# A retention layer and a squared-relu network in one kernel: the list scheduler that orders all instructions is given VectorE's rate beside GpSimd and new lags, and one constant is made elsewhere

## The chip, the cores and the metric

The kernel runs on one core of one Trainium2 chip. The metric is the device time of one execution in microseconds (us). A core has five engines with a queue of instructions each: PE (TensorE, matrix products), DVE (VectorE), ACT (ScalarE), POOL (GpSimd) and SP (SyncE, which here only issues DMA transfers). Each engine runs its own instructions in the order in which the program lists them, and waits on semaphores for those of others. PEld in the profile is TensorE's loading of weights, which overlaps its products. L12 is line 12 of the kernel.

## The reference

The inputs q, k and v have 8 batches, 8 heads, 576 positions and 64 dimensions, in fp32. What is computed:

```python
scores = scale * np.matmul(q, k.transpose(0, 1, 3, 2))
gamma = 1.0 - 2.0 ** (-5.0 - np.arange(H, dtype=np.float32))
rel = pos[:, None] - pos[None, :]
Dmat = np.where(rel >= 0, gamma[:, None, None] ** rel[None, :, :], 0.0)
attn_out = np.matmul(scores * Dmat[None, :, :, :], v)
x = np.ascontiguousarray(attn_out.transpose(0, 2, 1, 3)).reshape(B * S, H * D)
h = x @ w_in                  # 4608 x 512 by 512 x 2048
r = np.maximum(h, 0.0)
g = r * r
return (g @ w_out)            # 4608 x 2048 by 2048 x 512
```

So it is a retention layer (attention without softmax, with a decay per head that depends on the distance of two positions), followed by two dense layers with a squared relu between them. The output is 4608 x 512 in fp32.

## The kernel before, in words

**Tiles.** The 4608 tokens are cut into 36 units of 128. In each batch four "full" units cover positions 0 to 511; the last 64 positions of two batches together make one "tail" unit. Two units are a group, so there are 18 groups, and each group passes through the same stages.

**Retention.** The decay gamma^(i-j) is split in a factor of the row and one of the column, so that the positions of one unit can be treated as a small attention and everything earlier is carried in a state R of 64 x 64 per head. For each unit there are the scores psc (k against q, 64x64 products on TensorE), masked by VectorE into rx or rT; the sums psS (k and v multiplied into the next state), from which VectorE makes stmp, R and Rm; and the output psO, made of rx times v and of q times R. VectorE scales psO by gam_full into xT, which is the transposed input of the dense layers. v is scaled beforehand with vdec, a factor per position and head, into vx or v16. All these 64x64 products on TensorE have one line, L357.

**Loading.** Units 0 to 7 come as four pairs: 256 consecutive positions, with two positions in each of 128 partitions, so that a row of the transfer is two times 64 fp32 values, 512 B (L316, the transfer is called pair). VectorE, ScalarE and GpSimd cast a pair to fp16 (kx, qx and vx; L424 and L420), TensorE transposes kx and qx (psT, L439), and ScalarE or VectorE copies psT out as kqT (L450). In the text "second pair" is units 2 and 3, and the casts of a pair are named by its first unit (u == 2). From unit 8 on k, q and v are loaded singly (L298 to L304), GpSimd casts them (L371, L382, L387), and a DMA transfer on SP transposes k and q into kqT (L400). The weights w_in and w_out are loaded in four parts each, w0 to w3 and w4 to w7, issued by GpSimd's queue (L331) after v of the first pair has landed, and cast on the way.

**Dense layers.** The first, ph, is 16 tiles of 128 columns for each group, four products of 128x256 each, two tiles to a PSUM bank (L876). ScalarE takes the relu (rl, L884), and ScalarE or VectorE the square (gT, L894 and L896). The second layer of the first group is a plain sum over 16 tiles (L916). From the second group on it is computed by a scheme with seven block products instead of eight: VectorE forms four sums and differences of blocks of gT (gS, L946), TensorE multiplies them by blocks of w_out or by differences of such blocks (wT, made once on VectorE by L827), all in products po of 128x256 (L973). Copies of the partial results (p1, u2, u4) are made on ScalarE (L986), the outputs o are put together on VectorE (L996) and ScalarE, and SP stores them.

**What sets the order.** The program gives no order itself. Every piece of work is a task of the class Schedule: engine, key (a smaller key goes first), duration in us, the function that emits the instructions, the tasks it depends on, the buffers it takes (acq) and gives back (free), and a lag. The method emit plays the tasks forward with these durations. When an engine is free it takes the ready task with the smallest key whose buffers are there. The sequence of starts becomes the order of the instructions. So a duration or lag in the tables is not executed by anything, but decides what stands before what on each engine. DMA transfers are tasks of SP in one chain; each is given a duration and a time from its end to its landing (after). The weights are put in that chain too, though GpSimd issues them. LAG (a dict by transfer) adds to the time of landing that the order assumes.

The pieces near the change: make_vdec writes a vdl on VectorE and its exponential, vdec, on ScalarE. The decay of tail units needs a column iota_pt of 0 to 63 twice; make_tail_pool makes it by two GpSimd instructions from iota_p. It is a task of its own, and the casts of tail units wait for it by tail and gate. SQ_ACT names the ph tiles whose square runs on ScalarE; the others go to VectorE. The key of a dense-layer task is base + x, where base is 32 times the group's first unit.

Of the kernel before, what the change touches and what calls it, by code (L numbers as in the profile page):

```python
# [15 lines left out]
class Schedule:  # L16
# [7 lines left out]
    def add(self, eng, key, dur, fn, deps=(), acq=(), after=None, lag=0.0):  # L24
        t = dict(eng=eng, key=key, dur=dur, fn=fn, acq=acq, n=len(self.tasks), users=[], free=[], lag=lag,
                 left=len(deps), ready=0.0, lat=self.LAT[eng] if after is None else after)
        for d in deps:
            d["users"].append(t)
        self.tasks.append(t)
        return t  # L30
# [11 lines left out]
    def emit(self):  # L42
# [6 lines left out]
        def push(at, what, t):  # L49
            nonlocal seq  # L50
            seq += 1
            heapq.heappush(events, (at, seq, what, t))
# [3 lines left out]
        now = 0.0  # L56
        while True:
            for e in ready:
# [3 lines left out]
                while ready[e]:  # L62
                    item = heapq.heappop(ready[e])
                    t = item[2]
                    if all(self.count[r] >= t["acq"].count(r) for r in t["acq"]):
# [5 lines left out]
                        push(now + t["dur"], "end", t)  # L71
# [7 lines left out]
            while events and events[0][0] <= now + 1e-9:  # L79
                _, _, what, t = heapq.heappop(events)  # L80
                if what == "end":
                    busy[t["eng"]] = False
                    for w in t["users"]:

                        push(now + (0.0 if w["eng"] == t["eng"] else t["lat"]), "dep", w)
# [18 lines left out]
def kernel(  # L104
# [9 lines left out]
    nc = tc.nc  # L114
# [72 lines left out]

    iota_pair = const.tile([P, 2], FP32, name="iota_pair")
# [41 lines left out]
    BESIDE = 1.1  # L230
# [6 lines left out]
    LAG = {"k4": 0.7, "q4": 0.5}  # L237
# [24 lines left out]

    gate = {}

    def add_gated(eng, n, what, dur, fn):
        t = add(eng, -6 * L, dur, fn)
        gate.setdefault((what, n), []).append(t)
        return t

    def make_tail_pool():  # L270
        iota_pt = tile_of["iota_pt"] = const.tile([P, 1], FP32, name="iota_pt")
        nc.gpsimd.tensor_copy(out=iota_pt[0:64], in_=iota_p[0:64])
        nc.gpsimd.tensor_scalar(out=iota_pt[64:128], in0=iota_p[64:128], scalar1=-64.0, scalar2=None, op0=ALU.add)

    tail_pool = add_gated("POOL", 4, "v", 2.2, make_tail_pool)
    tail_dec = add("DVE", 0, 0.3, lambda: make_vdec("tail", tile_of["iota_pt"]), deps=[tail_pool])

# [47 lines left out]
    def add_weight(i):  # L325
# [10 lines left out]
        t = add("SP", 0, 2.75, lambda: None, deps=last_load + [issue], after=2.1 + LAG.get(f"w{i}", 0.0))  # L336
# [28 lines left out]
    def add_unit(u, base):  # L365

        kind, b, c = units[u]
        tail = [tail_dec] if kind == "tail" else []
# [23 lines left out]
        cv = add("POOL", base + 2, 1.1, fv, deps=[loaded["v", u]] + tail, acq=("v16",))  # L392
        for what, t in (("k", ck), ("v", cv)):
            for w in gate.get((what, u), []):
                sched.need(w, t)
# [7 lines left out]
    def add_unit_pair(u, base):  # L403
# [4 lines left out]
        for i, name in enumerate("kqv"):  # L408
            xs[name] = []
            for e in range(2):  # L410
                eng = ("DVE" if (e if name == "v" else lead) else "ACT" if name == "k" and u >= 4 or u == 2 and e else
                       "DVE" if name == "q" and u == 2 else "POOL")
# [288 lines left out]
    def after_sums(g, t, key, res):  # L701
# [24 lines left out]
        r2 = add("DVE", key + 0.3, 0.65, fr2, deps=[r1], acq=("R",))  # L726
# [95 lines left out]
    def add_wT(i, in0, in1):  # L822
        ts = []
        for h in range(2):
# [3 lines left out]
            ts.append(add("DVE", WT_KEY + i, 0.7, f, deps=sum((wcast[j] for j in range(4, 8 if i else 6)), [])))  # L828
# [6 lines left out]
    for x, y in ((t2, t1), (t4, t2)):  # L835
        for p in y:
            for w in x:
                sched.need(w, p)
# [19 lines left out]
    def add_ff(g):  # L858
# [10 lines left out]
        for fb in range(NF // nf):  # L869
# [18 lines left out]
            def fg(fb=fb, on_act=on_act):  # L888
# [6 lines left out]
                else:  # L895
                    nc.vector.tensor_tensor(out=t, in0=rl, in1=rl, op=ALU.mult)  # L896
            r = add("ACT", place(4 * fb + 4), 0.6, fr, deps=[f1[-1]], acq=("rl",))
            sched.free("ff", [r])
            sq.append(add("ACT" if on_act else "DVE", place(4 * fb + 6), 0.63 if on_act else 0.55, fg, deps=[r] + sq[:1],
                          acq=() if fb else ("g",)))  # L900
# [31 lines left out]
    def add_strassen(g, us, base, sq):  # L932
# [7 lines left out]
        def add_sum(k, key, parts, in0, in1, op, deps, start=()):  # L940
            out_ = []
            for h in range(parts):
# [4 lines left out]
                out_.append(add("DVE", key + h, (BESIDE if h else 0.5) if parts > 1 else 0.8, f, deps=deps(h, parts) + list(start)))  # L947
# [164 lines left out]
```

## Time and profile before

| quantity | value |
|---|---|
| median of five runs | 290.07 us (289.7, 289.73, 290.07, 290.97, 292.0) |
| the profiled execution, its own time | 290.07 us |
| its span on the core | 288.3 us |
| TensorE clock granted | 1.000 |
| TensorE (PE) busy | 281.0 us, 4346 products |
| weight loads of TensorE (PEld) busy | 236.2 us |
| VectorE busy | 176.7 us, 341 instructions |
| ScalarE busy | 187.6 us, 363 instructions |
| GpSimd busy | 86.5 us, 124 instructions |
| DMA packets | 122157, 94721 of them under 512 B, 49.94 MB in all |
| first product of the dense layers (ph) | 17.73 us |
| last product | ends at 283.3 us |

The span runs from the first to the last instruction on the core; the remaining 1.77 us of the execution lie around it. Busy times are sums over instructions of one engine in one execution. In a line of the profile such as "L827 DVE TENSOR_TENSOR wT<-w_out 128x1024" stand the line, the engine, the operation, and the tile written from the tile read, with partitions by elements. In the view of waits each line names the engine and line that waited, what it waited for, and then the sum, the number and the longest of the waits in us. In a timeline each line begins with the start and the duration in us, and the brackets at its end say how long the engine had been idle before and what ended that. Landings of transfers are taken from the completion records of the trace.

### The profile page before, as it was taken

The numbers are of one execution on the slowest core, as the hardware profiler recorded it, in microseconds if no ns is written. First come the engines' busy times: TensorE is split into PE (matmuls) and PEld (weight loads), VectorE is DVE, ScalarE is ACT, GpSimd is POOL, SyncE is SP. The second block draws the span as 40 slices with busy tenths as digits, with TensorE's granted clock in tenths as the row PEclk, the third lists the DMA queues.
The fourth block names the chain that finished last, engine by engine and source line by source line (L and its number), as shares of the span: only waits on it lengthen the run. The fifth ranks groups of instructions, "written<-read, shape, count | busy, mean of one in ns | idle before, by whom it ended". The sixth has DMA issues, their size and how long they took to land.

```text
span 288.3 us, 10135 instructions
## 1 busy us (share of the span) xinstructions
PE 281.0 (97%) x4346; PEld 236.2 (82%) x4346; DVE 176.7 (61%) x341; ACT 187.6 (65%) x363; POOL 86.5 (30%) x124
## 2 busy tenths in 40 slices
PE   7999999999999999999999999999999999999994
PEld 2578767888888888888888888888888888888883
DVE  3773379757566756647666564767566666364632
ACT  5559974667585857657576748675848665847830
POOL 5570035424415142524235241525343100000000
PEclk9999999999999999999999999999999999999999
DMA  7999999999999999998889898979889520102004
GB/s 197 276 208 206 246 290 259 134 257 162 206 207 187 217 198 218 186 217 167 208 168 219 211 175 193 214 190 238 187 173 206 129 75 5 73 2 75 0 2 146
DMA packets 122157, 49.94 MB, mean 173 GB/s; under 512 B 94721, under 2 KB 117761, under 8 KB 122113
## 3 DMA queue, kind: packets, MB, share of 16 engines
q1 hardware_dynamic: 117568, 44.84, 71.6%
q0 software_dynamic: 4224, 4.19, 8.8%
q8 instruction: 34, 0.56, 0.8%
q10 hardware_dynamic: 320, 0.26, 0.4%
q14 instruction: 11, 0.08, 0.1%
HBM read 36.70 MB, written 9.44 MB: 160 GB/s over the span
## 4 chain that ended last, share of the span: by engine, by line
PE 81%; DMA 10%; DVE 3%; SPq 2%; POOL 1%; issue 1%; DVEq 0%; POOLq 0%
PE ph L876 39%; PE po L973 35%; DMA pair<-in_v_dram 6%; DMA w_out<-in_moe_w_out_dram 5%; PE psO L357 4%; SPq L316 2%; PE psS L357 2%; PE psc L357 2%; DVE rx L490 1%; DVE wT L827 1%; DVE vx L420 1%; POOL vx L420 1%; DVE o L996 0%; DVE R L461 0%; POOL w_in L331 0%
## 5 line engine op out<-in xcount | busy, mean ns | idle before, releaser
L876 PE MATMUL ph<-xT,w_in 128*128 128x256 f16 x1152 | 136.4, 273 | 0.0
L876 PEld LDWEIGHTS <-w_in 128*128 128x128 f16 x1152 | 111.5, 98 | 14.2 <-issue 0.2
L884 ACT ACTIVATE rl<-ph 128x512 f16<-128x512 f32 x144 | 84.3, 587 | 49.9 <-PE ph L876 47.3
L894 ACT ACTIVATE gT<-rl 128x512 f16<-128x512 f16 x118 | 74.4, 631 | 3.4
L973 PEld LDWEIGHTS <-gS 128*128 128x128 f16 x544 | 51.7, 98 | 6.5
L973 PE MATMUL po<-wT,gS 128*128 128x256 f16 x408 | 55.8, 273 | 0.0
L973 PEld LDWEIGHTS <-gT 128*128 128x128 f16 x408 | 39.6, 98 | 4.7
L946 DVE TENSOR_TENSOR gS<-gT,gS 128x512 f16<-128x512 f16 (+1 forms) x51 | 28.7, 563 | 23.8 <-ACT gT L894 23.3
L973 PE MATMUL po<-w_out,gT 128*128 128x256 f16 x272 | 36.8, 273 | 0.0
L387 POOL TENSOR_TENSOR v<-v,vdec_full 128x512 f16<-128x512 f32 x24 | 27.4, 1143 | 26.7 <-DMA v<-in_v_dram 20.9
L371 POOL CAST kq<-k 128x512 f16<-128x512 f32 x28 | 18.2, 650 | 36.7 <-DMA k<-in_k_dram 31.3
L946 DVE TENSOR_TENSOR gS<-gT 128x1024 f16<-128x1024 f16 x34 | 24.3, 715 | 6.5 <-ACT gT L894 6.4
L896 DVE TENSOR_TENSOR gT<-rl 128x512 f16<-128x512 f16 x26 | 13.7, 525 | 20.7 <-ACT rl L884 20.7
L382 POOL CAST kq<-q 128x512 f16<-128x512 f32 x24 | 15.6, 649 | 34.8 <-DMA q<-in_q_dram 34.6
L996 DVE TENSOR_TENSOR o<-po,u 128x256 f32<-128x256 f32 x33 | 13.9, 421 | 15.6 <-PE po L973 7.8
L986 ACT COPY u<-po 128x256 f32<-128x256 f32 x34 | 12.5, 368 | 15.6 <-PE po L973 15.5
L751 DVE TENSOR_TENSOR xT<-psO,gam_full 128x512 f16<-128x512 f32 x28 | 18.0, 685 | 4.2 <-PE psO L357 4.2
L996 DVE TENSOR_TENSOR o<-po,p 128x256 f32<-128x256 f32 x18 | 7.6, 423 | 20.1 <-ACT u L986 13.3
L973 PE MATMUL po<-w_out,gS 128*128 128x256 f16 x136 | 18.0, 273 | 0.0
L973 PE MATMUL po<-wT,gT 128*128 128x256 f16 x136 | 17.6, 273 | 0.0
L692 DVE TENSOR_TENSOR rT<-psc,mask_full 128x512 f16<-128x512 f32 x24 | 15.6, 683 | 3.3 <-PE psc L357 3.1
L1047 ACT COPY o<-po 128x256 f32<-128x256 f32 x16 | 5.9, 370 | 11.1 <-PE po L973 10.8
(82 smaller groups left out, 228.0 us busy)
## 6 DMA issues: line engine op xcount, KB each, us to landing
out_dram<-o SPq DMA_DIRECT2D x32, 256.0 KB, 2.9
k<-in_k_dram SPq DMA_DIRECT2D x24, 256.0 KB, 4.5
q<-in_q_dram SPq DMA_DIRECT2D x96, 64.0 KB, 3.0
v<-in_v_dram SPq DMA_DIRECT2D x24, 256.0 KB, 3.6
pair<-in_k_dram SPq DMA_DIRECT2D x4, 512.0 KB, 5.9
pair<-in_q_dram SPq DMA_DIRECT2D x4, 512.0 KB, 7.1
pair<-in_v_dram SPq DMA_DIRECT2D x4, 512.0 KB, 7.8
w_in<-in_moe_w_in_dram POOLq DMA_DIRECT2D x4, 512.0 KB, 8.7
```

Source lines behind the costliest of these rows:

```text
L357: t = nc.tensor.matmul(out_, lhsT=lhsT, rhs=rhs, start=start, stop=True, skip_group_check=True, tile_position=(64 * row, 64 * col))
L371: op(out=out_.rearrange("p (n b a d) -> p n b a d", n=2, b=2, a=2), in_=in_.rearrange("p (a n b) d -> p n b a d", n=2, a=2))
L382: nc.gpsimd.tensor_copy(out=tile_of["kq", u][:, 1].rearrange("p (t a d) -> p a t d", t=4, a=2), in_=tile_of["q32", u].rearrange("p (a t) d ...
L387: nc.gpsimd.tensor_tensor(out=t, in0=tile_of["v32", u], in1=vdec[kind].rearrange("p (h o) -> p h o", o=1).to_broadcast([P, H, D]), op=ALU. ...
L692: tile_of["masking", g] = nc.vector.tensor_tensor(out=tile_of["rT", g][:, :, a], in0=tile_of["psc", g][a].rearrange("p (s n i) -> p s n i" ...
L751: nc.vector.tensor_tensor(out=tile_of["x", g].rearrange("p n (s e i) -> p e (n s) i", s=n, e=2)[:, c], in0=y.rearrange("p (o t r) -> p o r ...
L876: nc.tensor.matmul(tile_of["ph", g, fb][:, j, :], lhsT=w_in16[:, m, fi * P:(fi + 1) * P], rhs=tile_of["x", g][:, m, :], start=(m == 0), st ...
L884: nc.scalar.activation(out=t, in_=tile_of["ph", g, fb], func=ACTF.Relu)
L894: nc.scalar.activation(out=t, in_=rl, func=ACTF.Square)
L946: nc.vector.tensor_tensor(out=tile_of["S", g][:, k, sl], in0=in0(sl), in1=in1(sl), op=op)
L973: nc.tensor.matmul(tile_of["pb", g, bank], lhsT=left(i), rhs=right[:, i, :], start=(start and i == 0), stop=(i == HF - 1), skip_group_chec ...
L996: nc.vector.tensor_tensor(out=o_tile(u)[:, half * HM:(half + 1) * HM], in0=bank(x), in1=tile_of[name, g], op=ALU.add)
```

## The change

The operations of the kernel are the same but for three places, and the order of the rest is made anew.

- The scheduler knows a soft task. Tasks marked soft=True (VectorE's decay r2 of the state, the differences wT, VectorE's squares and the sums gS) are played at 0.22 of their rate while a GpSimd task of over 0.5 us runs (SHARED). Their durations are set to 0.43 or 0.72 for sums, 0.43 for squares, 0.68 for wT and 0.62 for r2; the constant BESIDE goes.
- Weights are played with 2.58 us each and 3.0 to landing instead of 2.75 and 2.1. LAG has eight entries instead of two.
- HURRY = 60 is taken off the keys of some tasks of the second group (g == 1): the relu of tile 7, the squares on VectorE, and the sums.
- The halves of wT depend on the half of w_out that they read, and the later differences on the same half of the earlier ones (zip).
- The column iota_pt is written by two GpSimd iotas among the constants, and make_vdec("tail") stands there too. The gate, make_tail_pool and the waits on them go.
- For the second pair ScalarE makes all four casts of k and q. Before, one cast of k was on GpSimd and one of q on VectorE.

Nothing in the diff touches the transfers of q, k and v of pairs, which have rows of 512 B in both. The new order that follows from these differs on TensorE mainly in the stretch that lay at 17 to 70 us, and at single places later. TensorE changes between 64x64 products and others 85 times in it instead of 81.

```diff
--- before.py
+++ after.py
@@ -21,8 +21,10 @@
         self.count = dict(count)
         self.tasks = []
 
-    def add(self, eng, key, dur, fn, deps=(), acq=(), after=None, lag=0.0):
-        t = dict(eng=eng, key=key, dur=dur, fn=fn, acq=acq, n=len(self.tasks), users=[], free=[], lag=lag,
+    SHARED = 0.22
+
+    def add(self, eng, key, dur, fn, deps=(), acq=(), after=None, lag=0.0, soft=False):
+        t = dict(soft=soft, eng=eng, key=key, dur=dur, fn=fn, acq=acq, n=len(self.tasks), users=[], free=[], lag=lag,
                  left=len(deps), ready=0.0, lat=self.LAT[eng] if after is None else after)
         for d in deps:
             d["users"].append(t)
@@ -54,6 +56,17 @@
             if t["left"] == 0:
                 heapq.heappush(ready[t["eng"]], (t["key"], t["n"], t))
         now = 0.0
+        port = dict(task=None, left=0.0, at=0.0, beside=False)
+
+        def shared(beside):
+            t = port["task"]
+            if t is not None:
+                port["left"] -= (now - port["at"]) * (self.SHARED if port["beside"] else 1.0)
+                port["at"] = now
+                t["end"] = now + max(port["left"], 0.0) / (self.SHARED if beside else 1.0)
+                push(t["end"], "end", t)
+            port["beside"] = beside
+
         while True:
             for e in ready:
                 if busy[e]:
@@ -68,7 +81,14 @@
                         t["start"] = now
                         order.append(t)
                         busy[e] = True
-                        push(now + t["dur"], "end", t)
+                        t["end"] = now + t["dur"]
+                        if t["soft"]:
+                            port.update(task=t, left=t["dur"], at=now)
+                            shared(port["beside"])
+                        else:
+                            push(t["end"], "end", t)
+                        if e == "POOL" and t["dur"] > 0.5:
+                            shared(True)
                         break
                     held.append(item)
                 for item in held:
@@ -79,7 +99,14 @@
             while events and events[0][0] <= now + 1e-9:
                 _, _, what, t = heapq.heappop(events)
                 if what == "end":
+                    if abs(t["end"] - now) > 1e-6:
+                        continue
+                    t["end"] = -1.0
                     busy[t["eng"]] = False
+                    if t["soft"]:
+                        port["task"] = None
+                    elif t["eng"] == "POOL" and t["dur"] > 0.5:
+                        shared(False)
                     for w in t["users"]:
 
                         push(now + (0.0 if w["eng"] == t["eng"] else t["lat"]), "dep", w)
@@ -185,6 +212,12 @@
         vdec[kind] = d
     make_vdec("full", iota_p)
 
+    iota_pt = const.tile([P, 1], FP32, name="iota_pt")
+    for s in range(2):
+        nc.gpsimd.iota(iota_pt[64 * s:64 * s + 64], pattern=[[0, 1]], base=0, channel_multiplier=1,
+                       allow_small_or_imprecise_dtypes=True)
+    make_vdec("tail", iota_pt)
+
     iota_pair = const.tile([P, 2], FP32, name="iota_pair")
     for s in range(2):
         nc.gpsimd.iota(iota_pair[64 * s:64 * s + 64], pattern=[[1, 2]], base=0, channel_multiplier=2,
@@ -227,14 +260,14 @@
     SQ_ACT = (0, 1, 2, 3, 4, 5, 6)
     SPREAD = 0.1
     QL = 0.8
-    BESIDE = 1.1
+    HURRY = 60
     PAUSE = 1.5
     PARTS = 1
     WT_KEY = 96
     URGENT = 40
     SQ_LATE = (1, 4, 6)
     JOIN = 5
-    LAG = {"k4": 0.7, "q4": 0.5}
+    LAG = {"k0": 0.3, "q2": 0.1, "w7": 1.4, "k4": 0.3, "q4": 0.7, "v4": 0.6, "q6": 0.3, "v6": 1.0}
     LAG_T, LAG_O = 1.5, 5.0
     PAIRED = 8
     FIRST = ["k0", "q0", "v0", "k2", "q2", "v2", "w0", "w1", "w2", "w3", "w4", "w5", "w6", "w7", "k4", "q4", "v4", "k6", "q6", "v6"]
@@ -259,21 +292,6 @@
         fill.append(add("PE", 10 ** 6, 1.75 if i == 0 else 0.43 if i < 15 else 0.216, warm, deps=fill[-1:], acq=() if fill else ("ff",)))
     sched.free("ff", fill[-1:])
 
-
-    gate = {}
-
-    def add_gated(eng, n, what, dur, fn):
-        t = add(eng, -6 * L, dur, fn)
-        gate.setdefault((what, n), []).append(t)
-        return t
-
-    def make_tail_pool():
-        iota_pt = tile_of["iota_pt"] = const.tile([P, 1], FP32, name="iota_pt")
-        nc.gpsimd.tensor_copy(out=iota_pt[0:64], in_=iota_p[0:64])
-        nc.gpsimd.tensor_scalar(out=iota_pt[64:128], in0=iota_p[64:128], scalar1=-64.0, scalar2=None, op0=ALU.add)
-
-    tail_pool = add_gated("POOL", 4, "v", 2.2, make_tail_pool)
-    tail_dec = add("DVE", 0, 0.3, lambda: make_vdec("tail", tile_of["iota_pt"]), deps=[tail_pool])
 
     def dma_task(key, dur, fn, **kw):
         t = add("SP", key, dur, fn, deps=list(last_load), **kw)
@@ -333,7 +351,7 @@
                 behind(tile_of["w", i], tile_of["load", "v", 0])
         issue = add("POOL", -90 + i, 0.9, fn, deps=issues[-1:] or [loaded["v", 0]], lag=1.0 if issues else 0.0)
         issues.append(issue)
-        t = add("SP", 0, 2.75, lambda: None, deps=last_load + [issue], after=2.1 + LAG.get(f"w{i}", 0.0))
+        t = add("SP", 0, 2.58, lambda: None, deps=last_load + [issue], after=3.0 + LAG.get(f"w{i}", 0.0))
         last_load[:] = [t]
         wcast[i] = [t]
 
@@ -365,7 +383,6 @@
     def add_unit(u, base):
 
         kind, b, c = units[u]
-        tail = [tail_dec] if kind == "tail" else []
 
         def sorted_cast(op, out_, in_):
             op(out=out_.rearrange("p (n b a d) -> p n b a d", n=2, b=2, a=2),
@@ -389,10 +406,7 @@
                 in1=vdec[kind].rearrange("p (h o) -> p h o", o=1).to_broadcast([P, H, D]), op=ALU.mult)
         ck = add("POOL", base, 0.65, fk, deps=[loaded["k", u]], acq=("kq",))
         cq = add("POOL", base + 1, 0.62, fq, deps=[loaded["q", u], ck])
-        cv = add("POOL", base + 2, 1.1, fv, deps=[loaded["v", u]] + tail, acq=("v16",))
-        for what, t in (("k", ck), ("v", cv)):
-            for w in gate.get((what, u), []):
-                sched.need(w, t)
+        cv = add("POOL", base + 2, 1.1, fv, deps=[loaded["v", u]], acq=("v16",))
         T["casts", u] = [ck, cq, cv]
         sched.free("ld", [ck, cq, cv])
         def fx2():
@@ -408,8 +422,7 @@
         for i, name in enumerate("kqv"):
             xs[name] = []
             for e in range(2):
-                eng = ("DVE" if (e if name == "v" else lead) else "ACT" if name == "k" and u >= 4 or u == 2 and e else
-                       "DVE" if name == "q" and u == 2 else "POOL")
+                eng = ("DVE" if (e if name == "v" else lead) else "ACT" if name == "k" and u >= 4 or u == 2 and name != "v" else "POOL")
 
                 def fc(name=name, e=e, eng=eng):
                     if (name + "x", u) not in tile_of:
@@ -723,7 +736,7 @@
         if not c0:
             T["Rread", g - 1].append(r0)
         r1 = add("DVE", key + 0.2 - URGENT, 0.69, fr1, deps=[r0])
-        r2 = add("DVE", key + 0.3, 0.65, fr2, deps=[r1], acq=("R",))
+        r2 = add("DVE", key + 0.3, 0.62, fr2, deps=[r1], acq=("R",), soft=True)
         T["Rm", g], T["R", g], T["Rread", g], T["Rmread", g] = r0, r2, [], r1
         sched.free("ff", [r0])
         sched.free("ff", [r1])
@@ -825,7 +838,7 @@
             def f(h=h):
                 sl = slice(h * HF // 2, (h + 1) * HF // 2)
                 nc.vector.tensor_tensor(out=wT[i][:, sl], in0=in0[:, sl], in1=in1[:, sl], op=ALU.subtract)
-            ts.append(add("DVE", WT_KEY + i, 0.7, f, deps=sum((wcast[j] for j in range(4, 8 if i else 6)), [])))
+            ts.append(add("DVE", WT_KEY + i, 0.68, f, deps=wcast[4 + h] + (wcast[6 + h] if i else []), soft=True))
         return ts
 
     t1 = add_wT(0, wB[0, 1], wB[0, 0])
@@ -833,9 +846,8 @@
     t3 = add_wT(2, wB[1, 1], wB[0, 1])
     t4 = add_wT(3, wB[1, 0], wT[1])
     for x, y in ((t2, t1), (t4, t2)):
-        for p in y:
-            for w in x:
-                sched.need(w, p)
+        for w, p in zip(x, y):
+            sched.need(w, p)
     wT_done = {7: t3, 6: t2, 5: t1, 4: t4}
 
     def store(u, o, lo=0, hi=DM, engs=(nc.sync, nc.sync)):
@@ -894,10 +906,10 @@
                     nc.scalar.activation(out=t, in_=rl, func=ACTF.Square)
                 else:
                     nc.vector.tensor_tensor(out=t, in0=rl, in1=rl, op=ALU.mult)
-            r = add("ACT", place(4 * fb + 4), 0.6, fr, deps=[f1[-1]], acq=("rl",))
+            r = add("ACT", place(4 * fb + 4) - HURRY * (g == 1 and fb == 7), 0.6, fr, deps=[f1[-1]], acq=("rl",))
             sched.free("ff", [r])
-            sq.append(add("ACT" if on_act else "DVE", place(4 * fb + 6), 0.63 if on_act else 0.55, fg, deps=[r] + sq[:1],
-                          acq=() if fb else ("g",)))
+            sq.append(add("ACT" if on_act else "DVE", place(4 * fb + 6) - HURRY * (g == 1 and not on_act), 0.63 if on_act else 0.43, fg, deps=[r] + sq[:1],
+                          acq=() if fb else ("g",), soft=not on_act))
             sched.free("rl", [sq[-1]])
         sched.free("x", [f1[-1]])
         base2 = base + NF * n
@@ -944,7 +956,7 @@
                     if ("S", g) not in tile_of:
                         tile_of["S", g] = stage.tile([P, 4, HF, P], FP16, name="gS", tag="wst")
                     nc.vector.tensor_tensor(out=tile_of["S", g][:, k, sl], in0=in0(sl), in1=in1(sl), op=op)
-                out_.append(add("DVE", key + h, (BESIDE if h else 0.5) if parts > 1 else 0.8, f, deps=deps(h, parts) + list(start)))
+                out_.append(add("DVE", key + h - HURRY * (g == 1), 0.43 if parts > 1 else 0.72, f, deps=deps(h, parts) + list(start), soft=True))
             sums[k] = out_
             return out_
         nb = len(sq) // 2
```

## The prediction

> **What bounds the kernel now.** I read the page's busy shares and chain first, then TensorE's waits, then a table by stretches of the span, then single stretches. Busy shares and chain:
>
> ```profile
> PE 281.0 (97%) x4346; PEld 236.2 (82%) x4346; DVE 176.7 (61%) x341; ACT 187.6 (65%) x363; POOL 86.5 (30%) x124
> PE 81%; DMA 10%; DVE 3%; SPq 2%; POOL 1%; issue 1%; DVEq 0%; POOLq 0%
> ```
>
> TensorE is busy 97% and is 81% of the chain; VectorE, which the change reorders, is 3%. TensorE's waits, longest first:
>
> ```profile
> PE warm L256 <- DVE wT L163: 1.3, 1, 1.3
> PE psS L357 <- POOL vx L420: 0.5, 1, 0.5
> PE psS L357 <- DVE vx L420: 0.4, 1, 0.4
> PE psT L439 <- DVE kx L424: 0.4, 1, 0.4
> ```
>
> The first, second and fourth fall before 11.3 us, among warm-up products. From the table by stretches (length, then busy us and counts of PE, PEld, DVE, ACT, POOL, granted clock, DMA share, GB/s):
>
> ```profile
> 0.00:20.00 20.00, 17.70 (x255) 9.79 (x256) 13.57 (x54) 9.74 (x22) 13.57 (x34) 1.00 1.05 228
> 40.00:60.00 20.00, 19.45 (x368) 16.06 (x366) 16.50 (x28) 13.83 (x28) 9.20 (x12) 1.00 1.08 222
> 80.00:120.00 40.00, 40.00 (x681) 34.81 (x679) 26.31 (x46) 27.16 (x53) 14.47 (x19) 1.00 1.02 202
> 160.00:200.00 40.00, 40.00 (x667) 34.91 (x667) 24.66 (x43) 27.63 (x53) 14.99 (x19) 1.00 0.93 194
> ```
>
> TensorE has no gap from 80 us on. The only loss after the first useful product (ph, 17.73 us) is in 40 to 60. The timeline there:
>
> ```profile
> 48.28 1.09 DVE L420 TENSOR_TENSOR vx<-pair,vdec_pair 128x512 f16<-128x512 f32 x1
> 48.83 0.22 PE L357 MATMUL psS<-vx,kx 64*64 64x64 f16 x4
> 49.43 0.41 PE L357 MATMUL psS<-vx,kx 64*64 64x64 f16 x28 [0.38 <-DVE vx L420]
> ```
>
> The gap is 0.38 here; by the spacing of the matmuls it costs 0.57, and another 0.14 at 50.5. So the removable loss is **0.71 us** in all. TensorE then runs to 283.3; the last sums and stores take it to 288.3. The profiled execution took 290.07, 1.77 outside the span, and is equal to the median of the runs shown (290.07), so changes to the sum carry over as they are.
>
> **What the Trainium skill says.** "SBUF — State Buffer", SBUF: two separate sides: VectorE and GpSimd share a port pair as an exclusive lock held for a whole instruction, the loser blocked. The trace agrees: VectorE's vx takes 0.69 alone and 1.09 above, beside GpSimd; its sums gS (two forms) run from 0.41 to 1.15. That is what the new model copies. "TensorEngine Tiling (Array Packing)", Key Properties: changing the tiling mode drains TensorE. The trace agrees: each visit to the 64x64 products of L357 between full products costs about 0.2 us over its matmuls, 0.1 a switch. "Perfetto Trace Analysis", Identifying the Most-Contended Engine: optimize the most occupied engine first, and don't read TensorE's busy share as closeness to its peak; here the shares only tell me that no waits are left to remove. "DMA: Bandwidth & Descriptors", Specifications, puts line rate at transfers of 512 B or more; 94721 of 122157 packets are smaller, and the change's lines leave all of those as they are.
>
> **The change, part by part.**
>
> *Rows of pairs.* Both kernels load k, q and v of pairs by the same statement (L316), 2x64 fp32 or 512 B a row. Cost nothing: no transfer differs.
>
> *Tail constant.* GpSimd's COPY (0.18) and TENSOR_SCALAR (0.22) go; two iotas enter earlier (0.35 for two in the row of iota_pair). VectorE's 0.23 and ACT's 0.30 stay. In before, kx of the first pair waited in VectorE's queue behind this until 5.87, though k had landed at 5.17: up to 0.66 for that cast. But the next cast, qx, waits for q, landed 6.98, and starts at 7.00; the first ph waits for the first weights, landed 17.23 (17.73 after the 32 psc matmuls of 17.15). Worth 0. Were both covers gone it would be worth 0.66; in the other direction GpSimd has 2.5 us of room before v lands at 8.79.
>
> *Casts of the second pair.* One k cast leaves GpSimd and one q cast VectorE; ACT does four of 0.62: 10.62 to 11.86, and after q lands at 12.4, 12.43 to 13.67. The copies kqT behind them on ACT end by about 16.7, ahead of psc at 17.15. Worth 0, with 0.4 us of cover.
>
> *TensorE's order.* The same 4346 matmuls, but another sequence. Full-array and 64x64 products alternate 85 times instead of 81; four switches at 0.1: **+0.40**, all before 53 us (eight visits between 17.7 and 52 instead of six).
>
> *Weights.* Landings are unchanged (issued by GpSimd once v of the first pair has landed): w3 24.86, w4 27.39, w5 30.44, w6 32.47, w7 35.31. In the new order the visit of 20.89 comes at 20.0, behind 20 ph products instead of 28. Walking on at 109 ns for 128x256 and 216 for 128x512: the ph that needs w3 is reached at 24.60 and starts at 24.90 (+0.30); the po that needs w5 is reached at 30.12 and starts at 30.50 (+0.37). Before, these had 0.10 and 0.27 to spare. **+0.67**. Queued behind them is only TensorE's own stream. From 30.5 no weight is late.
>
> *Pairs three and four.* The transfers (k 36.9, q 38.7, v 40.5, then 42.3, 44.0, 45.5) don't move: k of pair 3 is still tied to w5's landing. ACT and VectorE cast in a new order; VectorE now ends vx of the last pair at about 47.7 (rx to 46.2, stmp and R to 47.0, vx 0.7), and the psS that takes it comes at 48.8. The 0.71 goes: **-0.71**. Late next: nothing; R and rx have some 0.5 us to spare.
>
> *Rates, HURRY, LAG, wT by halves.* These issue nothing: they only place instructions. In the steady state gS, rT and xT had 0.45 us or more to spare and ACT's copies u about 0.30 (product end, 0.2, copy 0.37, against 0.87 of other product). I find no new wait: 0. If a u copy slipped by one relu (0.59), each group so placed would lose about 0.3.
>
> *Transposes (L400).* In the same stretch the scores of four groups move earlier in TensorE's stream, by the matmuls now placed behind them: psc of 85.6, 98.4, 111.8 and 125.0 by 1.34, 1.34, 1.78 and 2.22 us. They take kqT, transposed by DMA while the DMA share is at 1.02. In before:
>
> ```profile
> 105.69 1.39 SPq L400 DMA_TRANSPOSE kqT<-kq  x1
> 111.83 0.43 PE L357 MATMUL psc<-kqT 64*64 64x64 f16 x32
> DMA to landing us min/median/max: 3.1/4.6/5.6
> ```
>
> This transpose landed at 111.10, 5.41 after its issue, as all DMA queues stood still for some 1.65 around 108.8 (they do five times in this run). The four landings were 84.86, 97.27, 111.10 and 122.73. With TensorE at -0.04 (0.67 - 0.71), the psc would come at 84.2, 97.1, 110.0 and 122.7: if transposes land as before, waits of 0.65, 0 (after that shift), 0.45 and 0, **1.1**. If they land earlier, as one transfer fewer stands ahead of the first and the standstill may fall elsewhere, 0. I take the middle, **+0.55**. Upper bound 2.2, with one more standstill in a bad place. Below nothing is excluded: a landing can't speed up TensorE, which doesn't wait for it now.
>
> Sum: 0.40 + 0.67 - 0.71 + 0.55 = +0.91: 290.07 + 0.91 = **291.0**.
>
> **The rivals.**
> *A, waits vanish, nothing new.* If ph work fills in for w3 and w5 (they land 0.3 earlier) and no transpose is late: 0.40 - 0.71 = -0.31, **289.8**. For it: landings are DMA times that vary, and the waits are short. Against: weights issue at the same place, and their slack was only 0.10.
> *B, no effect.* The switches and weights cancel against the vx wait: +0.36 and no transposes, or less: **290.1 to 290.4**. For it: TensorE's 40.00 of 40.
> *C, the other side: transposes become the bound.* Scores of 85 to 125 us come up to 2.22 earlier and their margins were 0.7, 1.2, 0.7 and 2.2. With landings as before and one standstill of 1.65 less 0.55 of cover: 0.36 + 1.1 + 1.1 = +2.56, **292.6**. It decides against the old time as soon as TensorE waits more than 1.1 us there, and past the bound of measurement then. For it: the DMA share above 1 until 120. Against: loads ahead of the transposes can move up too.
> A gain over 0.5% needs 1.45 us; only 0.71 of waiting is there.
>
> **How the numbers follow.** 0.5% (1.45 us, about what a measurement of this kernel can tell from no change) puts the limits at 288.6 and 291.5. Forecast 0.45 (290.4 to 291.6, some 0.10 of it past 291.5), A 0.13, B 0.14, C 0.24 (of it 0.22 past), something unseen 0.04. So faster 0.04, same 0.61, slower 0.35. The likeliest gives 291.0; the range, with A's and most of C, is 289.7 to 292.4.
>
> **What would show it.** Right: no TensorE wait for vx after 17.7; short waits for DMA w_in or w_out near 24.6 and 30.1; psc at 84, 97 and 110 waiting on DMA kqT; 40.00 of 40 later on. Wrong: waits of TensorE on VectorE (gS, R) or ACT (u) that return in every group, in either direction of the new rates; a first ph later than 17.73; a landing of the weights that has moved, as GpSimd's queue issues them; or a last group whose tail from 283.3 is longer.

## The result, and the profile after

| | before | changed |
|---|---|---|
| median | 289.93 us (76 runs) | 290.64 us (39 runs, 289.88 to 292.16) |
| ratio to before | 1 | 1.0024, 95% interval 1.0015 to 1.0033 |
| profiled execution, span | 290.07, 288.3 us | 290.47, 288.8 us |

The forecast was 291.0, with "the same within 0.5%" as the likeliest outcome; the kernel is slower by 0.7 us, or 0.24%. Busy shares, chain and TensorE's waits of the changed kernel:

```profile
PE 281.0 (97%) x4346; PEld 235.6 (82%) x4346; DVE 176.4 (61%) x340; ACT 188.1 (65%) x365; POOL 88.1 (31%) x123
PE 77%; DMA 12%; SPq 5%; ACT 2%; POOL 2%; issue 1%; DVE 0%; DVEq 0%; POOLq 0%; ACTq 0%
```

```profile
PE warm L289 <- DVE wT L190: 1.3, 1, 1.3
PE psS L375 <- POOL vx L433: 1.0, 2, 0.7
PE psT L452 <- DVE qx L437: 0.5, 1, 0.5
PE psc L375 <- DMA kqT<-kq: 0.2, 1, 0.2
```

Two lines are new after 17.7 us: one of the two waits for GpSimd's vx (of pair 3, near 42 us), and the wait for a transposed kqT. DMA has gone from 10 to 12% of the chain. By stretches of the span (columns as in the prediction):

```profile
0.00:20.00 20.00, 17.31 (x253) 9.49 (x254) 13.65 (x54) 10.69 (x24) 13.22 (x33) 1.00 1.06 229
40.00:60.00 20.00, 19.45 (x358) 15.35 (x357) 16.12 (x28) 12.93 (x26) 9.34 (x12) 1.00 0.96 220
80.00:120.00 40.00, 39.76 (x678) 34.62 (x677) 26.09 (x45) 26.33 (x52) 14.73 (x19) 1.00 0.93 201
160.00:200.00 40.00, 40.00 (x631) 34.80 (x628) 25.92 (x42) 29.12 (x57) 15.85 (x19) 1.00 0.93 202
```

The stretch of 40 to 60 is as it was, 19.45, though its old wait is gone, and 80 to 120 has lost 0.24. The timeline of the two places:

```profile
40.64 0.69 DVE L433 TENSOR_TENSOR vx<-pair,vdec_pair 128x512 f16<-128x512 f32 x1 [2.34 <-DMA pair<-in_v_dram]
40.78 1.45 POOL L433 TENSOR_TENSOR vx<-pair,vdec_pair 128x512 f16<-128x512 f32 x1 [0.63 <-ACT gT L906]
42.28 0.45 PE L375 MATMUL psS<-vx,kx 64*64 64x64 f16 x32 [0.37 <-POOL vx L433]
...
105.48 1.71 SPq L414 DMA_TRANSPOSE kqT<-kq  x1
...
110.10 0.30 PE L375 MATMUL psc<-kqT 64*64 64x64 f16 x16
110.64 0.32 PE L375 MATMUL psc<-kqT 64*64 64x64 f16 x16 [0.24 <-DMA kqT<-kq]
```

v of pair 3 lands at 40.62. GpSimd's half of vx takes 1.45 us beside VectorE's half, and psS, which stood at 42.76 before, is now reached at 41.9. The same two lines in the kernel before:

```profile
40.70 1.45 POOL L420 TENSOR_TENSOR vx<-pair,vdec_pair 128x512 f16<-128x512 f32 x1 [0.65 <-ACT o L923]
42.76 0.45 PE L357 MATMUL psS<-vx,kx 64*64 64x64 f16 x32
```

So GpSimd's half ended at 42.15 there, ahead of psS. The scores of one group are reached at 110.1; the second half of them waits for a kqT that lands at 110.6. The standstill of the DMA queues that the prediction saw at 108.8 is there again: from 108.0 to 109.5 they moved 12 GB/s, against 243 in the 1.5 us before.

An account of TensorE makes the comparison exact. "Spacing" is the time from the start of one matmul to the start of the next. From the first ph to the start of the last product I sum it in three parts: products by the full array; stays at 64x64 products (a "visit", with its switch on either side); and what goes beyond the usual spacing, a wait. Before, those pauses are 0.57 and 0.14 for vx, as predicted, and three of 0.11 to 0.15 near 104, 170 and 214 us, which I had passed over. After, they are 0.18 and 0.15 (weights), 0.44 (vx), 0.43 (kqT), and 0.05 (the transposes psT near 40 us).

| us | before | changed | difference |
|---|---|---|---|
| full-array products | 238.65 | 238.70 | +0.05 |
| visits, without waits | 26.41 (35 of them) | 26.84 (37) | +0.43 |
| waits | 1.10 | 1.25 | +0.15 |
| sum | 266.16 | 266.79 | +0.63 |

The tail after the last product is 0.14 shorter. The span so differs by 0.5, the medians by 0.7. The clock granted was 1.000 and 0.998 in the two profiles; the full-array products take the same time in both, so the clock is not the cause.

### The profile page after: what moved, and what is told of

The parts are those of the page before. It is cut to its first block, busy times and chain, and to the rows that moved or that the text cites. A ratio compares the mean times of both kernels' runs of the same rounds, so it can differ in the third digit from the quotient of the medians.

```text
span 288.8 us, 10135 instructions
## 1 busy us (share of the span) xinstructions
PE 281.0 (97%) x4346; PEld 235.6 (82%) x4346; DVE 176.4 (61%) x340; ACT 188.1 (65%) x365; POOL 88.1 (31%) x123
## 4 chain that ended last, share of the span: by engine, by line
PE 77%; DMA 12%; SPq 5%; ACT 2%; POOL 2%; issue 1%; DVE 0%; DVEq 0%; POOLq 0%; ACTq 0%
PE ph L888 36%; PE po L985 34%; DMA w_out<-in_moe_w_out_dram 5%; PE psO L375 4%; DMA pair<-in_v_dram 3%; DMA pair<-in_k_dram 2%; SPq L322 2%; SPq L334 2%; PE psc L375 2%; DMA kqT<-kq 2%; PE psS L375 2%; POOL vx L433 1%; DMA v<-in_v_dram 1%; ACT rl L896 1%; ACT gT L906 1%
## 5 line engine op out<-in xcount | busy, mean ns | idle before, releaser
L958 DVE TENSOR_TENSOR gS<-gT,gS 128x512 f16<-128x512 f16 (+1 forms) x51 | 32.1, 629 | 21.5 <-ACT gT L906 21.0
L404 POOL TENSOR_TENSOR v<-v,vdec_full 128x512 f16<-128x512 f32 x24 | 25.8, 1073 | 26.8 <-DMA v<-in_v_dram 23.6
L388 POOL CAST kq<-k 128x512 f16<-128x512 f32 x28 | 21.2, 759 | 37.1 <-DMA k<-in_k_dram 33.0
L399 POOL CAST kq<-q 128x512 f16<-128x512 f32 x24 | 16.3, 678 | 26.5 <-DMA q<-in_q_dram 26.3
L908 DVE TENSOR_TENSOR gT<-rl 128x512 f16<-128x512 f16 x26 | 11.9, 458 | 18.1 <-ACT rl L896 18.0
L985 PE MATMUL po<-w_out,gS 128*128 128x256 f16 x136 | 17.7, 273 | 0.0
```

Source lines behind the costliest of these rows:

```text
L388: op(out=out_.rearrange("p (n b a d) -> p n b a d", n=2, b=2, a=2), in_=in_.rearrange("p (a n b) d -> p n b a d", n=2, a=2))
L399: nc.gpsimd.tensor_copy(out=tile_of["kq", u][:, 1].rearrange("p (t a d) -> p a t d", t=4, a=2), in_=tile_of["q32", u].rearrange("p (a t) d ...
L404: nc.gpsimd.tensor_tensor(out=t, in0=tile_of["v32", u], in1=vdec[kind].rearrange("p (h o) -> p h o", o=1).to_broadcast([P, H, D]), op=ALU. ...
L958: nc.vector.tensor_tensor(out=tile_of["S", g][:, k, sl], in0=in0(sl), in1=in1(sl), op=op)
L985: nc.tensor.matmul(tile_of["pb", g, bank], lhsT=left(i), rhs=right[:, i, :], start=(start and i == 0), stop=(i == HF - 1), skip_group_chec ...
```

## The experiments

The theory (in the texts below "theory of the stream") is that the time is TensorE's products, visits and waits, and that the new order has two visits more and other waits than before. The rival ("contention") is that VectorE and GpSimd block each other more: in the first row of gS on the page these sums take 32.1 us instead of 28.7. Ratios are to the kernel before, run on the same chip in turn.

### What a visit costs: e4 and e15

e4 puts one full-array product inside a visit and so cuts it in two; e15 puts the same product in front of the visit, where it cuts nothing.

```diff
--- before
+++ e4_split, in emit_scores, for each of the two units s of a group
+            if s:
+                nc.tensor.matmul(tile_of["psc", g][0][:, 256:384], lhsT=ident, rhs=ident, start=True, stop=True, skip_group_check=True)
             ps = [x[:, cols(s)].rearrange("p (n i) -> p n i", i=64) for x in tile_of["psc", g]]
--- before
+++ e15_product_no_split (likewise at the start of emit_scores where groups are not joined)
+    def beside(g):
+        nc.tensor.matmul(tile_of["psc", g][0][:, 256:384], lhsT=ident, rhs=ident, start=True, stop=True, skip_group_check=True)
...
             def f1():
+                tile_of["psc", g + 1] = banks("psc")
+                beside(g + 1)
                 emit_out1(g)
                 emit_scores(g + 1)
```

> The kernel before with one product of 128x128 by the full array put between the two units' scores in all 14 groups from unit 8 on; its result is overwritten by the scores that follow. It cuts each of these visits in two. Theory of the stream: 14 times (0.056 for the product and 0.22 for the further visit) is +3.9, about 293.8. Rival, that a visit costs nothing beyond its matmuls: 14 times 0.056, +0.8, 290.7.

> The control of e4_split: the same 14 products of 128x128, but each ahead of the visit, where TensorE is at full-array products anyway. Its result is overwritten too. Theory of the stream: 14 times 0.056, +0.8, 290.7. If the product itself was what cost in e4, +4.1 again, 294.

e4: 294.05 us (before 289.95), ratio 1.0149 (1.0131 to 1.0166), +4.1. e15: 290.97 (before 290.31), ratio 1.0034 (1.0017 to 1.0051), +0.7. One cut visit in the timeline of e4:

```profile
87.42 0.30 PE L357 MATMUL psc<-kqT 64*64 64x64 f16 x16
87.65 0.23 PE L617 MATMUL psc<-ident 128*128 128x128 f16 x1
87.81 0.32 PE L357 MATMUL psc<-kqT 64*64 64x64 f16 x16
```

By the spacing, an uncut visit of 48 products takes 0.602 us, and the same cut in two 0.471 and 0.354 without the added product: 0.223 for the cut. So 14 times 0.223 and 14 times 0.056 is 3.9 of the 4.1. The price of a further visit is shown; two more of them in the changed kernel make 0.44, and 0.43 was found.

### Which part makes the loss: e2, e16, e3 and e8

```diff
--- changed
+++ e2_old_times (and e16)
-    LAG = {"k0": 0.3, "q2": 0.1, "w7": 1.4, "k4": 0.3, "q4": 0.7, "v4": 0.6, "q6": 0.3, "v6": 1.0}
+    LAG = {"k4": 0.7, "q4": 0.5}
-        t = add("SP", 0, 2.58, lambda: None, deps=last_load + [issue], after=3.0 + LAG.get(f"w{i}", 0.0))
+        t = add("SP", 0, 2.75, lambda: None, deps=last_load + [issue], after=2.1 + LAG.get(f"w{i}", 0.0))
--- before
+++ e3_new_weights: the second pair of lines the other way round; e8_both_times: both pairs
```

> The changed kernel with the assumed times of transfers undone (weights 2.75 and 2.1 to landing, LAG of two entries); rates, HURRY, halves of wT, casts and constant stay as changed. It has 33 visits instead of 37, and the scores of 85 to 111 us stand where the kernel before has them. Theory of the stream: four visits less is -0.88; no wait for a transposed kqT near 110 us (-0.4); the psS of the last pair stands where it stood before, so its wait for vx is back (+0.6); weights wait 0.3 as now. Sum about -0.7, 289.9. It says the loss is in the assumed times of the transfers, not in VectorE's rates. Rival, contention or rates: no better than the changed kernel, 290.6.

> The kernel before with one part of the change alone: the assumed times of the weights (2.58 and 3.0). It has 36 visits instead of 35, with psS of pair 3 and the scores of 85 to 111 us earlier still than in the changed kernel. Theory of the stream: one visit +0.22, weights +0.3, psS of pair 3 waits 0.5 to 1.1 for GpSimd's vx, kqT +0.4 or more, and the waits for vx of the last pair (0.71) go; sum +0.7 to +1.3, 290.6 to 291.2: this part alone makes the whole loss. Rival, rates of VectorE: 289.9, as before.

> The kernel before with the assumed times of the weights and the new LAG, the old rates, casts, constant and keys. 36 visits. If LAG repairs what the weights' times spoil in e3 (292.4), it is near the changed kernel, 290.6 to 291.0. If rates and HURRY repair it, it stays at 292. I expect between: psS of pair 3 at its place in the changed kernel (-0.3), w5 no wait (-0.4), the wait for gS stays: 291.6.

> e2_old_times once more, beside e13 on the same chip: 289.7, that is between no difference and 0.2% under the kernel before.

| | rates, HURRY, casts, constant, halves of wT as before | as changed |
|---|---|---|
| assumed times of transfers as before | 1 (before) | 1.0004 (0.9988 to 1.0019), again 0.9996 (0.9964 to 1.0028) |
| new | 1.0057 (1.0038 to 1.0075) (e8) | 1.0024 (the changed kernel) |

Each ratio is to the kernel before in the same series of runs. The loss is in the assumed times of transfers. With the old ones, VectorE's new rates and all else make no difference that can be measured (289.68 against 289.95 in e2, 290.57 against 290.31 in e16). With the new ones alone the kernel is slower by 0.57%, and what else the change does takes about half of that back. e3, the weights' times without LAG, is at 292.37, ratio 1.0090 (1.0070 to 1.0110), worse than I expected. With LAG (e8) it is less, though the two intervals just overlap. Its waits:

```profile
PE psS L357 <- POOL vx L420: 1.1, 2, 0.7
PE po L973 <- DVE gS L946: 0.7, 1, 0.7
PE psc L357 <- DMA kqT<-kq: 0.5, 1, 0.5
PE po L916 <- DMA w_out<-in_moe_w_out_dram: 0.2, 1, 0.2
```

A weight and a transpose are steps of the prediction; vx of pair 3 and the gS are not. e8 is at 291.79, near the 291.6 expected, but partly by luck: psS of pair 3 doesn't wait at all, w5 is waited for after all (0.36 by the spacing), and in place of gS there is a pause of 0.62 at 50.25, which comes up again in e7, beside 0.87 for a kqT. In e2, with 33 visits, the view lists only this after 17.7 us (by the spacing some pauses of 0.1 to 0.3 stand beside it):

```profile
PE psS L375 <- POOL vx L433: 0.2, 1, 0.2
```

The rival in its plain form falls: e2 has the new rates and isn't slower, e3 has the old ones and is. Nor does the time follow the sums: over all forms gS takes 51.3 us of VectorE in the kernel before and 54.4 in the changed one, but 55.4 in e2, which isn't slower, and 53.2 in e7 (next), which is slower than the changed kernel.

### What HURRY takes back: e7

```diff
-    HURRY = 60
+    HURRY = 0
```

> The changed kernel with HURRY = 0: the sums and squares of the second group get no precedence on VectorE. 37 visits as in the changed kernel. e3 (new weights alone) waited 0.74 us for gS near 46 us; if HURRY is what took that wait away, it is back: 291.3. Rival, that HURRY does nothing: 290.6.

291.90 us, ratio 1.0069 (1.0050 to 1.0087): without HURRY the changed kernel is 0.45% slower, about e8. So HURRY does most of the repair, or all of it. The wait that came was not the gS that I named. The timeline:

```profile
50.12 0.37 ACT L998 COPY u<-po 128x256 f32<-128x256 f32 x1 [1.81 <-PE po L985]
50.55 0.60 PE L985 MATMUL po<-w_out,gS 128*128 128x256 f16 x4 [0.46 <-ACT u L998]
```

A product now stands directly behind the one whose result ScalarE must copy out first (0.62 by the spacing). A pause of the same length, before a product of the same kind (w_out with gS), stands at 50.25 in e8, which has no HURRY either; the view puts it down to VectorE's o there, which ends 0.04 after the copy u. None of the runs that have HURRY shows it. The profile of e7 has 1.15 us for a kqT near 123 besides.

### Taking the found losses out of the changed kernel: e1, e5, e6 and e14

Tasks got a tag; after the order is made, each pair of MOVES puts a task, with those that depend on it, directly behind another.

```diff
+        for tag, behind in MOVES:
+            x = next(t for t in order if t["tag"] == tag)
+            y = next(t for t in order if t["tag"] == behind)
+            i, j = order.index(x), order.index(y)
+            late = [x]
+            for t in order[i + 1:j + 1]:
+                if any(t in d["users"] for d in late):
+                    late.append(t)
+            assert y not in late
+            order[i:j + 1] = [t for t in order[i:j + 1] if t not in late] + late
+# tags: ("psS", unit), ("psO1", unit), ("psc", unit, half), ("po", group, product, quarter), ("ph", group, bank, tile), ("out1", group)
+# e1: MOVES = [(("psS", 4), ("po", 1, 7, 0)), (("psc", 4, 0), ("po", 1, 7, 1)), (("psS", 4), ("po", 1, 7, 1)), (("psS", 6), ("po", 1, 5, 1))]
+# e5: the first three, (("psO1", 4), ("po", 1, 5, 1)), (("psS", 6), ("ph", 2, 0, 1))
+# e6: e5 and (("out1", 5), ("ph", 4, 4, 1)), (("out1", 6), ("po", 4, 5, 3)), (("out1", 7), ("po", 5, 5, 3)), (("out1", 8), ("po", 6, 6, 3))
+# e14: e6 and (("kx", 4, 0), ("square", 1, 6)), (("vx", 4, 1), ("gS", 1, 3, 0))
```

> The changed kernel, with four of TensorE's tasks moved and every other engine's order kept: for pair 3 the sums psS and both halves of the scores psc stand together (one visit to 64x64 products instead of three), for pair 4 psS stands beside the first half of psc. So 34 visits after the first dense product instead of 37, and psS of pair 3 comes about 1.0 us later in TensorE's stream. Theory of the stream (the time is TensorE's products, its visits at 0.22 us each and its waits): three visits less is -0.66, the wait of 0.44 for GpSimd's vx goes, sum -1.1, about 289.5, under the kernel before. Rival, contention (the change is slower because VectorE and GpSimd now block each other more: the sums gS take 32.1 us instead of 28.7): the orders of those two are the same as in the changed kernel, so no difference to it, about 290.6.

290.81 us, ratio 1.0032 (1.0020 to 1.0044): no gain, as the rival had it, but not for its reason. The wait for vx of pair 3 is gone and three visits are saved, 1.1 us in all. Most of that is lost 5 us further on:

```profile
46.82 0.42 DVE L487 TENSOR_TENSOR R<-stmp,dec 128x256 f16<-128x256 f32 x1
46.95 0.63 PE L388 MATMUL psO<-kqT,R 64*64 64x128 f16 x6
48.07 0.24 PE L388 MATMUL psO<-kqT,R 64*64 64x128 f16 x2 [0.48 <-issue]
```

TensorE is at psO earlier, and the last two products wait for R, which VectorE ends at 47.24: 0.70 by the spacing, and 0.16 ahead of it. Three pauses of 0.12 to 0.16 near 91, 102 and 216 us take another 0.45 in this execution.

> The changed kernel with five of TensorE's tasks moved: for pair 3 psS and both halves of psc in one visit as in e1_join, its psO behind three more product tasks (so that R, which e1 waited 0.7 us for, is there) and directly before the first half of psc of pair 4, and psS of pair 4 beside the second half. 33 visits instead of 37. Theory of the stream: -0.88 for visits, -0.44 for GpSimd's vx, no wait for R: 289.3 if transposes are in time. But the scores near 110 us then come 1.3 us earlier against a landing that need not move; if landings are fixed, half or all of that is waited for: 289.3 to 290.6. Rival, contention of VectorE and GpSimd: as the changed kernel, 290.6, without a wait for kqT.

290.40 us, ratio 1.0021 (1.0009 to 1.0033). 33 visits, but psO waits for R again (0.48), the next group's ph for xT (0.37), and a weight costs 0.32.

> e5_tuned, and the visits with the scores of four groups (those near 83, 96, 109 and 122 us) each moved behind four more products tasks or two tiles of ph, about 0.9 to 1.3 us later in TensorE's stream, about where the kernel before has them. Theory of the stream with late transposes: no wait for kqT, 289.2, faster than the kernel before (289.9) by 0.2%. If transposes weren't late in e5 it is as e5. Rival, contention: 290.6.

290.12 us, ratio 1.0012 (0.9999 to 1.0025). No wait for kqT is left in its profile; the interval doesn't part it from e5 or from before. What it waits for:

```profile
PE ph L901 <- DVE xT L603: 0.6, 1, 0.6
PE psT L465 <- DVE qx L450: 0.4, 1, 0.4
PE po L941 <- DMA w_out<-in_moe_w_out_dram: 0.3, 1, 0.3
```

How little of the removed work arrives can be seen at one visit that has the same products ahead of it in all three, psO of pair 4. The line is that of the changed kernel, of e5 and of e6:

```profile
55.20 0.64 PE L375 MATMUL psO<-rx,vx 64*64 64x128 f16 x32
```

```profile
54.83 0.64 PE L388 MATMUL psO<-rx,vx 64*64 64x128 f16 x32
```

```profile
54.73 0.64 PE L388 MATMUL psO<-rx,vx 64*64 64x128 f16 x32
```

Four visits (0.88) and a wait (0.44) were taken out ahead of it, and it comes 0.4 to 0.5 earlier. Between 40.6 and 49.5 us VectorE has no gap in these kernels: vx when v of pair 3 lands, three gS, R, four rx, stmp, R, vx, two xT. The gS among them take 1.27, 0.68 and 0.68, the first of them beside GpSimd's vx. In e6 psS is done at 43.05, but VectorE starts R only at 43.65, behind these sums. So a weaker rival remained: in this stretch VectorE's chain sets the time.

> e6_tuned_scores_later, and ScalarE makes the square of tile 6 of the second group before it casts k of pair 3, and VectorE makes its three sums gS before its half of vx of pair 3 and not behind it. In e6 VectorE had no gap from 40.6 to 49.5 us and one gS took 1.27 us beside GpSimd's vx; TensorE waited 0.76 us for xT and came out where e2 does not wait. If the gS behind vx are what makes that chain late, it starts 0.5 us earlier and the xT wait shrinks: 289.5 to 289.7. Rival: the chain is set by the landing of v (40.6) and by psS and psc, and xT comes no earlier: as e6, 290.1.

290.89 us, ratio 1.0014 (0.9988 to 1.0041), no gain over e6 that can be measured. Its profiled execution is a long one (span 293.4, with 3.8 us of waits for kqT after 84 us), so I read only the stretch in question, the four rx, in e6 and then in e14:

```profile
43.98 2.47 DVE L516 TENSOR_TENSOR rx<-psc,mask 128x512 f16<-128x512 f32 x4
```

```profile
43.93 2.48 DVE L516 TENSOR_TENSOR rx<-psc,mask 128x512 f16<-128x512 f32 x4
```

The rx start no earlier, as the rival of this run had it, but its reason is not shown. In e14:

```profile
40.64 1.16 POOL L446 TENSOR_TENSOR vx<-pair,vdec_pair 128x512 f16<-128x512 f32 x1 [0.62 <-DMA pair<-in_v_dram]
40.82 1.53 DVE L971 TENSOR_TENSOR gS<-gT,gS 128x1024 f16<-128x1024 f16 x1
42.27 0.68 DVE L446 TENSOR_TENSOR vx<-pair,vdec_pair 128x512 f16<-128x512 f32 x1
42.95 0.47 PE L388 MATMUL psS<-vx,kx 64*64 64x64 f16 x32
```

GpSimd's half of vx is now done at 41.80, but VectorE's half stands behind a sum that takes 1.53 beside GpSimd's, and ends at 42.95, where psS starts (42.60 in e6). So the edit only put one cause of the delay in place of another. Whether the landing of v alone would set the time of this stretch stays open.

### A version meant to beat both: e13

```diff
--- e2_old_times
+++ e13_old_times_joined
+MOVES = [(("psS", 6), ("po", 1, 3, 3))]
```

> e2_old_times with one of TensorE's tasks moved: psS of pair 4 stands directly before the second half of psc, four product tasks later, so that GpSimd's vx (waited for 0.2 us in e2) is there. 33 visits as in e2. Theory of the stream: -0.2 to e2, 289.5, which is 0.15% under the kernel before. If the sums that follow from psS become late instead (R is needed by psO of pair 4 some 5 us later, so I don't expect it), no gain.

290.80 us (before 290.31), ratio 1.0005 (0.9979 to 1.0031): no gain that can be measured. None of the kernels here beats the one before clear of the interval.

## Why the prediction was right

- **Start** (0 for constant and casts of the second pair): right. The first ph is at 17.73 in both.
- **TensorE's order** (+0.40): right, +0.43, and the price of 0.2 per visit is shown by e4 and e15.
- **Weights** (+0.67): mis-sized. The trace has +0.33, and only 0.15 of it comes from the new order. The ph for w3 waited 0.15 where I had 0.30. The po for w5 waited nothing, as w5 landed some 0.4 earlier in this execution (k of pair 3, tied to it, was issued at 30.08 and not at 30.58). The other 0.18 is the ph for w1, which I had not counted and which stands at about 19.5 in both orders: w1 landed at 19.36 in the profile before and at 19.62 in the one after. e15 has the old order there, w1 lands at 19.58, and the wait is 0.15.
- **Pairs three and four** (-0.71): the wait for vx of the last pair went. The step that failed is its sentence "Late next: nothing". psS of pair 3 comes 0.9 earlier in the stream, v lands when it did, and GpSimd's half of vx ends at 42.24: +0.44. The prediction has a price only for VectorE's half of a vx (0.69, or 1.09 in the line that it shows). GpSimd's half pays when VectorE's starts first: 1.45 for pair 3 in both kernels, against 1.04 for the last pair. The profile before had that line too (40.70, above).
- **Rates, HURRY, LAG** (0): right in that no wait returns in every group. The three pauses of 0.11 to 0.15 us in the steady state went, -0.39, which was not in the sum. That the change removed them is not shown: e1, with the change's rates, has three such pauses, and e15, with the old ones, one of 0.16 at 130. That HURRY is worth 0.45% here, and hides most of what the weights' times cost, was not seen.
- **Transposes** (+0.55, from 0 to 2.2): right in kind, in place for one of two: +0.43 at 110 us. At 84 us kqT landed at 83.26, in time for 84.41. The 0.55 was the middle between 1.1 and 0, so the near hit says little: e1, with the same order there, has 0.09 at 110 and 0.39 near 123.

The predicted sum was +0.91, the trace has +0.63, the medians +0.71. That these lie so near each other is in part luck: the vx that was not counted (+0.44) and the pauses that went (-0.39) cancel. The visits, w3, the two vx and kqT alone give 0.43 + 0.15 - 0.71 + 0.44 + 0.43 = 0.74, of which only the price of the visits is free of the spread between executions (the wait of 0.71 for vx is 0.45 in e15). Rival A needed weights and transposes in time (they cost 0.33 and 0.43) and no new wait for vx; rival C needed transposes as late as before, and the one due at 84.4 landed 1.6 earlier (83.26 against 84.86).

Three figures given before the result are off, without effect on the argument. The last product of the kernel before starts at 283.89 and ends at 284.16, not 283.3. TensorE changes between 64x64 products and others 80 times before and 84 after; 81 and 85 count the stretches between. The chances of the parts add up to 0.64 for the same and 0.32 for slower, not 0.61 and 0.35.

## What to carry to other kernels

When one engine is full, look at what its stream gets more of (here visits, 0.22 us each) and at each wait that a moved task can meet. Price a wait by the slower of the engines that share the work. Taking out a wait saves little if the engine behind it is no earlier; the wait then reappears at the next consumer, as in e1, where TensorE waited for R of VectorE instead. A scheduler's assumed times are worth testing apart from each other: here one half of the change cost 0.57% and the other half took back about half of that.

## What the runs showed of the hardware

A stay at 64x64 products between full-array products costs 0.22 us beyond its matmuls (e4 against e15). Where VectorE and GpSimd worked beside each other, the one that started second took longer in the cases read here: GpSimd's half of vx took 1.45 started 0.14 behind VectorE's half, and 1.04 for the last pair; a sum of VectorE took 1.53 started 0.18 behind GpSimd's vx (e14), and 0.68 otherwise.

Two executions of one kernel (e2 and e16, on two chips) took 289.24 and 292.02 us at nearly the same clock (0.999 and 0.998). Full-array products sum to 238.63 and 238.65 us in them; the whole 2.8 us are waits of TensorE. It is not the chip alone: the executions of e16 on its one chip run from 289.32 to 293.45. The waits of the slower one:

```profile
PE psc L375 <- DMA kqT<-kq: 0.7, 2, 0.4
PE psS L375 <- DVE vx L433: 0.7, 1, 0.7
PE psS L375 <- POOL vx L433: 0.4, 1, 0.4
PE ph L888 <- DMA w_in<-in_moe_w_in_dram: 0.3, 1, 0.3
```

v of the last pair landed at 46.19 in one and at 47.56 in the other, the third part of w_in at 22.08 and 23.14. Of the 1.37 for v, 0.49 is a later issue (40.68 and 41.17): SP waited for GpSimd's cast of q, which ended at 40.65 and 41.15. The rest is the transfer's own. So an order whose margins to landings are some tenths of a microsecond can lose them to transfers and to what holds up their issue, and a single profile, such as the one that the prediction's 0.10 and 0.27 were read from, tells the landings only to about a microsecond.
